# Retention then gated feed-forward: where the third and fourth parts of w_in stand in the hand-written opening

## The chip, the cores and the metric

The kernel runs on one core of one Trainium2 chip. The metric is the device time of one execution in microseconds (us). The kernel before takes 1028.38 us, the median of five runs (1027.11 to 1031.23).

## The reference

```python
# q, k, v: (8 batches, 8 heads, 576 tokens, 64), fp32
scores = q @ k.T / sqrt(64)
ret    = scores * Dmat           # Dmat[i, j] = gamma_h ** (i - j) for i >= j, else 0
x      = ret @ v                 # laid out as (4608 tokens, 512 = heads * 64)
h      = x @ w_in                # w_in: (512, 2048), float64
g      = h * erf(softplus(h))
out    = g @ w_out               # w_out: (2048, 512), float64; out in fp32
```

## The kernel before

**Attention by pieces.** The 4608 tokens are cut into 36 pieces of 128. They are counted from 0 here, as in the code, so "the sixth piece" is piece 5. A piece goes through three stages. `transposes(i)` (L315), here Ti, turns q and then k on TensorE against `ident` (into `pt_q`, `pt_k`, L332), has ScalarE copy both to SBUF (`qT`, `kT`), has GpSimd weigh v (L313), and asks for q of piece i+2. `scores(i)` (L341), here Si, multiplies k by q (L347), and VectorE masks the result into `sT`. `outputs(i)` (L354), here Oi, multiplies `sT` by v (L365), adds what earlier pieces of the batch left (L376), forms the new state (L388), has VectorE scale and sum (`x`, `sums`) and GpSimd scale the state (L427), and asks for k and v of piece i+3. A load of q, k or v of one piece is two DMAs of 128 KB (L147), so a piece is 768 KB.

**Feed-forward by chunks.** Four pieces make a chunk of 512 tokens. The first chunk is multiplied by the first group of w_in columns in the plain way: `plain()` (L539) has 16 steps, four for each quarter of the 512 rows of w_in, and a step is four matmuls (L550, into `p`, `p`, `pe`, `pg`). The steps of a quarter need the part of w_in with these rows, already rounded. Later chunks use a Strassen-like scheme (L496, L604).

**Weights.** w_in and w_out come as float64 words. `load_weights()` (L232) asks for the next part: of w_in, 512 KB in two DMAs of 256 KB on SyncE's queue (L237), into one of four buffers `wraw`. `round_weights(n)` takes n steps of `rounding()` (L240), which turns one part into fp32 in `wa`. The first step is two instructions on ScalarE (L254, L255), the next three are one instruction each on VectorE (L259, L263, L267), and the fifth is three (L272, L274, L275), on VectorE too for the first group of w_in. So "5" rounds one part.

**Queues.** Each engine runs its instructions in the order in which the code issues them, and SyncE issues its DMAs in that order; nothing is rescheduled. Eight completion semaphores go round among the DMAs, so that a DMA's issue also waits for the landing of the one eight before it.

**The opening.** A string of letters drives the first chunk (L727): "a" runs the next attention stage, "w" asks for a part of the weights, a digit takes so many rounding steps, "p" is one step of `plain()`, "k" issues two matmuls that keep TensorE busy, and "l", "c", "s" are a load, the rest of the constants and a store of x. With the stages and parts written out, the kernel before runs:

```
T0 l k S0 k T1 k O0 w1 k S1 k T2 k O1 w2 S2 T3 3 O2 w3 w4 S3 2 T4 O3 S4 5 pp T5 pp O4 w5 w6 pp S5 5 pp
O5 w7 5 T6 pp w8 c pp S6 5 pp T7 O6 S7 pp 5 s
```

"3" and "2" round part 1; the following "5"s round parts 2, 3, 4, 5 and 6 (w5 on belongs to w_out). T3 asks for q of piece 5 and O2 for its k and v.

Of the kernel before, what the change touches and what calls it, by code (L numbers as in the profile page):

```python
# [54 lines left out]
def kernel(  # L55
# [94 lines left out]
    def load(i, names="qkv"):  # L150
        if i < len(pieces):
            t = loaded.setdefault(i, {})
            for name in names:
                src = {"q": q, "k": k, "v": v}[name]
                if name == "q" and i < SQUARES:
                    t["q"] = load_rows(i, "q", q, 2)
                elif name == "q":
                    t["qs"] = load_squares(i, "q", q)
                    if i >= SQUARES_K:
                        t["ks"] = load_squares(i, "k", k)  # L160
                elif name == "v" or i < SQUARES_K or len(pieces[i]) == 1:
                    t[name] = load_rows(i, name, src, 4)
# [69 lines left out]
    def load_weights():  # L232
        part = next(coming, None)
        if part is not None:
            t = wraw.tile([P, 2 * WP], UINT32, tag="wraw", name="wraw")
            for rows, src in part[0]:
                nc.sync.dma_start(out=t[rows].rearrange("p (h f) -> p h f", h=2), in_=src)  # L237
            words.append((t, *part[1:]))
# [49 lines left out]
    def round_weights(n=1):  # L288
        for _ in range(n):
            next(round_step, None)  # L290
# [159 lines left out]
    def attend(upto):  # L450
        while done[0] < min(upto, len(stages)):
            of, i = stages[done[0]]
            of(i)
            done[0] += 1
# [9 lines left out]
    def store_x(c):  # L464
        nc.sync.dma_start(out=xd[c], in_=x[0, c][:, :n_dc])
# [242 lines left out]
    def keep_busy(n):  # L708
        for _ in range(n):
            nc.tensor.matmul(idle[:, :P], lhsT=ones, rhs=ones, start=True, stop=True)  # L710
# [13 lines left out]

    for what in "alkakakawkakakawaa3awwa2aaa5ppappawwppa5ppaw5appwcppa5ppaaapp5s":  # L727
        if what == "a":
            attend(done[0] + 1)
        elif what == "p":  # L730
            next(products)
        elif what == "s":
            store_x(0)
        elif what == "l":
            load(2, "kv")
        elif what == "c":
            nc.sync.dma_start(out=cst[:, CONST_FIRST:], in_=consts[:, CONST_FIRST:])
        elif what == "w":
            load_weights()
        elif what == "k":  # L740
            keep_busy(2)
        else:
            round_weights(int(what))
# [93 lines left out]
```

## Time and profile before

| what | value |
|---|---|
| median of five runs | 1028.38 us |
| the profiled execution's own time | 1027.11 us |
| its span in the profile | 1025.3 us |
| TensorE busy | 1017.5 us, 99% of the span |
| VectorE, ScalarE, GpSimd busy | 65%, 38%, 12% |
| granted TensorE clock | 0.999 |
| DMA | 165.76 MB, mean 162 GB/s |

Times in the views are counted from the start of the span. 1.81 us of the profiled execution's time lie outside its span. "Busy" is the time that an engine spends in instructions; the timeline joins equal instructions into one row with its start, its length and, in brackets, how long the engine sat idle before it and what ended that. A row of TensorE (PE) that is longer than others of its kind hides a wait between its instructions. SPq is the issuing of DMAs by SyncE; a DMA lands some us after its issue.

### The profile page before, as it was taken

How to read it: one execution, taken by the hardware profiler on the slowest of the kernel's cores; microseconds unless marked ns; L12 is line 12 of the kernel's file. 1: busy time of each engine (PE TensorE's matmuls, PEld its weight loads, DVE VectorE, ACT ScalarE, POOL GpSimd, SP SyncE). 2: the span in 40 equal slices, each digit the busy share in tenths (PEclk: the TensorE clock that was granted, in tenths of full speed). 3: DMA queues.
4: the chain of work that ended last, by engine and by line, in shares of the span. 5: the costliest groups of instructions: out<-in, count | busy, mean ns of one | idle time of the engine just before them, and what ended most of it. 6: DMA issues, size and time to landing. Idle time of an engine off the chain costs nothing.

```text
span 1025.3 us, 15950 instructions
## 1 busy us (share of the span) xinstructions
PE 1017.5 (99%) x6348; PEld 876.2 (85%) x6348; DVE 669.6 (65%) x1055; ACT 390.4 (38%) x481; POOL 123.4 (12%) x122
## 2 busy tenths in 40 slices
PE   9999999999999999999999999999999999999998
PEld 8787888888788888888888888888888888888887
DVE  3869777977976656656666666666567655555555
ACT  2354133233234444434343444444433333333332
POOL 2143112122312110010001001000100000000000
PEclk9999999999999999999999999999999999999999
DMA  9997989979984344544444345444433334444433
GB/s 196 205 252 165 232 194 224 250 150 251 245 191 159 111 156 145 167 159 154 166 142 165 123 147 164 162 144 144 144 124 124 125 130 132 125 134 136 124 95 112
DMA packets 146986, 165.76 MB, mean 162 GB/s; under 512 B 97376, under 2 KB 121568, under 8 KB 138848
## 3 DMA queue, kind: packets, MB, share of 16 engines
q1 hardware_dynamic: 144848, 163.70, 57.0%
q10 hardware_dynamic: 2064, 1.05, 0.4%
q8 instruction: 50, 0.82, 0.4%
q14 instruction: 24, 0.20, 0.1%
HBM read 117.52 MB, written 47.19 MB: 161 GB/s over the span
## 4 chain that ended last, share of the span: by engine, by line
PE 83%; DMA 6%; DVE 4%; SPq 4%; issue 1%; ACT 1%; POOL 1%; ACTq 0%; DVEq 0%; POOLq 0%
PE a L604 23%; PE a L496 22%; PE g L604 11%; PE g L496 11%; PE e L604 6%; PE e L496 5%; DMA raw_v<-in_v_dram 2%; PE o L365 2%; PE s L347 2%; SPq L131 2%; SPq L147 1%; DMA wraw<-in_moe_w_in_dram 1%; DMA raw_ks<-in_k_dram 1%; PE o L388 1%; PE o L376 1%
## 5 line engine op out<-in xcount | busy, mean ns | idle before, releaser
L496 PE MATMUL a<-x,wa 128*128 128x256 f32 x1088 | 258.3, 380 | 0.0
L496 PEld LDWEIGHTS a<-x,wa 128*128 128x128 f32 x1088 | 205.8, 190 | 28.5
L604 PE MATMUL a<-wb,s 128*128 128x256 f32 x864 | 205.7, 381 | 0.0
L604 PEld LDWEIGHTS a<-wb,s 128*128 128x128 f32 x864 | 162.9, 190 | 23.5 <-ACT o L618 0.7
L99 DVE TENSOR_TENSOR t<-g,t 128x512 f32<-128x512 f32 x68 | 46.9, 690 | 150.4 <-ACT t L526 112.8
L496 PE MATMUL g<-x,wa 128*128 128x256 f32 x544 | 129.2, 380 | 0.0
L496 PEld LDWEIGHTS g<-x,wa 128*128 128x128 f32 x544 | 102.8, 190 | 14.4
L99 DVE TENSOR_TENSOR o<-a,o 128x512 f32<-128x512 f32 x108 | 74.1, 686 | 49.3 <-PE a L604 49.3
L521 ACT COPY t<-a 128x512 f32<-128x512 f32 x34 | 19.9, 585 | 188.2 <-PE a L496 188.2
L99 DVE TENSOR_TENSOR t<-t,s 128x1024 f32<-128x1024 f32 x72 | 88.9, 1274 | 0.0
L565 ACT ACTIVATE s<-t 128x1024 f32<-128x1024 f32 x72 | 72.1, 1049 | 27.4 <-DVE t L99 27.4
L274 POOL TENSOR_TENSOR wraw<-wraw 128x512 f32<-128x512 f32 x28 | 29.4, 1050 | 440.2 <-DVE wraw L272 178.1
L99 DVE TENSOR_TENSOR x<-x 128x512 f32<-128x512 f32 x115 | 75.8, 692 | 1.2
L532 ACT COPY t<-a 128x512 f32<-128x512 f32 x34 | 19.9, 586 | 144.4 <-PE a L496 144.4
L569 ACT ACTIVATE s<-s 128x1024 f32<-128x1024 f32 x72 | 72.1, 1049 | 0.4
L604 PE MATMUL g<-wb,s 128*128 128x256 f32 x288 | 68.6, 381 | 0.1
L604 PE MATMUL e<-wb,t 128*128 128x256 f32 x288 | 68.5, 381 | 0.0
L604 PE MATMUL a<-wb,t 128*128 128x256 f32 x288 | 68.5, 381 | 0.0
L604 PE MATMUL g<-wb,t 128*128 128x256 f32 x288 | 68.2, 380 | 0.0
L496 PE MATMUL e<-x,wa 128*128 128x256 f32 x272 | 64.8, 381 | 0.0
L99 DVE TENSOR_TENSOR o<-g,o 128x512 f32<-128x512 f32 x72 | 49.2, 683 | 23.6 <-ACT o L618 18.8
L99 DVE TENSOR_TENSOR sT<-s,cst 128x512 f32<-128x512 f32 x72 | 46.1, 681 | 27.9 <-PE s L347 27.9
(76 smaller groups left out, 1227.6 us busy)
## 6 DMA issues: line engine op xcount, KB each, us to landing
od<-o SPq DMA_DIRECT2D x54, 512.0 KB, 3.3
x<-xd SPq DMA_DIRECT2D x27, 1024.0 KB, 4.8
o<-od SPq DMA_DIRECT2D x27, 1024.0 KB, 5.0
raw_qs<-in_q_dram SPq DMA_DIRECT2D x96, 112.0 KB, 4.3
raw_ks<-in_k_dram SPq DMA_DIRECT2D x84, 112.0 KB, 4.2
xd<-x SPq DMA_DIRECT2D x9, 1024.0 KB, 5.4
raw_v<-in_v_dram SPq DMA_DIRECT2D x64, 128.0 KB, 4.5
wraw<-in_moe_w_in_dram SPq DMA_DIRECT2D x32, 256.0 KB, 5.6
```

The source lines that it names most:

```text
L99: nc.vector.tensor_tensor(out=out, in0=in0, in1=in1, op=op)
L131: nc.sync.dma_start(out=t[part * SQ : (part + 1) * SQ, :, at : at + m - SQ], in_=tokens[:, :, d0 : d0 + m - SQ])
L147: queue.dma_start(out=t[r0 : r0 + n, e::2, :], in_=heads.rearrange("h p d -> p h d"))
L274: engine.tensor_tensor(out=r_f, in0=high_f, in1=r_f, op=ALU.mult)
L347: nc.tensor.matmul(ps[e][:, p, :], lhsT=t["kT"][heads[e], p, :], rhs=t["qT"][heads[e], p, :], start=True, stop=True)
L365: nc.tensor.matmul(o[p % 2][heads[(e + p) % 2], p // 2, :], lhsT=t["v"][:, 2 * p + e, :], rhs=t["sT"][:, e, p, :], start=(p < 2), stop=(no ...
L496: nc.tensor.matmul(acc[:, j * TH : (j + 1) * TH], lhsT=weights["wa", self.g][:, a, d, j * P : (j + 1) * P], rhs=x[self.g, self.c][a][:, d, :],
L521: nc.scalar.copy(out=self.t1[:, 1], in_=self.a)
L532: nc.scalar.copy(out=self.t2[:, 0], in_=self.a)
L565: nc.scalar.activation(self.s[:, j], t, AF.Softplus)
L569: nc.scalar.activation(self.s[:, j], self.s[:, j], AF.Erf)
L604: nc.tensor.matmul(acc[:, tp, :], lhsT=left[:, j * TH + tp * P : j * TH + (tp + 1) * P], rhs=weights["wb", self.g][:, b, j, :], start=(sta ...
```

## The change

Only the string changes.

```diff
-    for what in "alkakakawkakakawaa3awwa2aaa5ppappawwppa5ppaw5appwcppa5ppaaapp5s":
+    for what in "alkakakawkakakawwaa3awa2aaa5ppappa5wwppa5ppawappwcppa5ppaaapp5s":
```

Written out, the kernel after runs:

```
T0 l k S0 k T1 k O0 w1 k S1 k T2 k O1 w2 w3 S2 T3 3 O2 w4 S3 2 T4 O3 S4 5 pp T5 pp O4 5 w5 w6 pp S5 5 pp
O5 w7 T6 pp w8 c pp S6 5 pp T7 O6 S7 pp 5 s
```

On SyncE's queue the two DMAs of w3 move ahead of the six of piece 5; w4 stays where it was, behind v of piece 5 and ahead of piece 6. On VectorE the rounding of part 3 moves ahead of the masking of S5, and that of part 4 ahead of the scaling of O5. TensorE, ScalarE and GpSimd run the same instructions in the same order as before.

## The prediction

> **What bounds the kernel now.** I read the page first. Its line on the engines settles that TensorE is the bound: it idles for under 8 of 1025.3 us.
>
> ```profile
> PE 1017.5 (99%) x6348; PEld 876.2 (85%) x6348; DVE 669.6 (65%) x1055; ACT 390.4 (38%) x481; POOL 123.4 (12%) x122
> ```
>
> So this change can only take away a wait of TensorE or add one. Next the table of waits for the first 100 us, in which the change lies: line, what was waited for, us in total, times, longest.
>
> ```profile
> PE p L550 <- DVE wa L275: 1.1, 2, 0.8
> ...
> PE s L347 <- DVE qT L326: 0.4, 1, 0.4
> ```
>
> The matmuls of the first chunk wait twice, 1.1 us together, for a rounded part of w_in. The timeline of TensorE says where.
>
> ```profile
> 29.55 1.99 PE L550 MATMUL p<-x,wa 128*128 128x256 f32 x8
> 31.38 0.60 PE L332 MATMUL pt_q<-ident,raw_q 128*128 128x128 f32 x4
> 31.88 0.63 PE L332 MATMUL pt_k<-ident,raw_k 128*128 128x128 f32 x4
> 32.34 1.03 PE L550 MATMUL pe<-x,wa 128*128 128x256 f32 x4
> ...
> 36.03 1.99 PE L550 MATMUL p<-x,wa 128*128 128x256 f32 x8 [0.30 <-DVE wa L275]
> ...
> 40.97 1.09 PE L365 MATMUL o<-sT,raw_v 128*64 128x128 f32 x16
> ...
> 49.60 1.99 PE L550 MATMUL p<-x,wa 128*128 128x256 f32 x8 [0.75 <-DVE wa L275]
> ```
>
> The wait at 36.03 is for part 2, which the change doesn't touch; the one at 49.60 is for part 4. The rows at 31.38 and 31.88 are T5. Its last input is the second DMA of k of piece 5. The timeline of SyncE's queue gives the issues; under them is, from the answer on this tile for the two DMAs of the second row, the time from issue to landing.
>
> ```profile
> 24.98 1.09 SPq L147 DMA_DIRECT2D raw_q<-in_q_dram  x2
> 26.12 1.05 SPq L147 DMA_DIRECT2D raw_k<-in_k_dram  x2
> ```
>
> ```profile
> DMA to landing us min/median/max: 5.1/5.1/5.1
> ```
>
> The second k DMA is issued at 26.67 and, at 5.1 us, lands at 31.8. T5 uses it at 31.88: no slack, and no wait to be seen either, since the matmuls of 29.55 end just before.
>
> **Part by part: the DMA that moves.** w3 (512 KB) goes ahead of q, k and v of piece 5 (768 KB). In this stretch the queue lands its DMAs in the order of issue, at 166 to 226 GB/s by the table of windows, with five or more on the way, so what w3 takes is added to q and k. How much, the parts show. Behind w2 the landings are: w2's second at 29.8 (issue 23.18, 6.6 us), w3's second at 37.0 (31.45, 5.5), w4's second at 39.7 (32.74, 6.9). Before w2, v of piece 4 landed at 27.6 (22.04, 5.5), and before w3 v of piece 5 at 33.4 (29.25, 4.2). So a part takes 2.2 us (w2), 3.6 (w3, asked for late) or 2.7 (w4, straight behind w3). The moved w3 will stand straight behind w2, as w4 stands behind w3: I take 2.7 and keep 2.2 to 3.6. k of piece 5 lands at 34.5 and T5's transposes of k start at 34.6, not 31.88: **+2.7 us**. TensorE runs in order, and behind T5 stand `pe` and `pg`, O4, and all the rest; no other work fills the hole. Later DMAs keep their places: w4 and piece 6 follow as before, and piece 6 had slack (k landed at 41.8, T6 used it at 43.7).
>
> The Trainium skill, "DMA: Bandwidth & Descriptors", section "Specifications", gives 358 GB/s from HBM per core. By that 512 KB would take 1.5 us and the sum below would be 1.2 us smaller; the windows here stay well below it (166 to 226 GB/s), so the row decides.
>
> **The waits that go.** With TensorE 2.7 us later, part 2 is ready in time: **-0.3**. Part 4's rounding now comes before O5's scaling, and at 49.60 it is over long since: **-0.75**. Nothing is late in its place: S6 stands just ahead on TensorE, and its own inputs (T6) are old.
>
> **VectorE's new order.** Here is what the rounding of part 3 costs, and the masking it now precedes (timeline of VectorE).
>
> ```profile
> 36.56 0.41 DVE L99 TENSOR_TENSOR x<-o,cst 128x256 f32<-128x256 f32 x1
> 39.15 1.29 DVE L99 TENSOR_TENSOR sT<-s,cst 128x512 f32<-128x512 f32 x2 [2.18 <-PE s L347]
> 40.35 0.41 DVE L259 TENSOR_SCALAR wa<-wa 128x512 f32<-128x512 f32 x1
> ...
> 43.25 0.69 DVE L275 TENSOR_TENSOR wa<-wa,wraw 128x512 f32<-128x512 f32 x1
> 43.86 0.42 DVE L99 TENSOR_TENSOR x<-o,cst 128x256 f32<-128x256 f32 x1
> ```
>
> The six instructions take 3.5 us (40.35 to 43.86). In the new order they begin after O4's scaling. O4 ends 2.7 us later than before, at 38.4, its scaling at 39.2 (two instructions of 0.41 after it); ScalarE has done part 3's share by then (behind T5's copies, at 36.9). So the rounding fills 39.2 to 42.7, most of which VectorE idled before (2.18 us), and `sT` of S5 comes at 42.7 to 44.0. O5 (40.97, now +2.4) is due at 43.4 and needs both halves, so its second matmul waits until 44.0: **+0.6**. The nearest rows are O2 and O3, where `sT` came 0.36 and 0.49 us after the start and the 16 matmuls took 1.51 and 1.64 us for 1.09. Bounds: 0 to 1.0. Part 4 then fills 44.0 to 47.5; it delays O5's scaling to 48.4, and behind that waits S6, for its PSUM buffers, at 50.6: cover of 2 us. GpSimd's state and the weighing of v of piece 6 move to 48 to 50; O6 needs them at 54.5. ScalarE's two instructions a part keep their order and are short of nothing. If w3 came later than 39, the rounding would push `sT` further, us for us; at 32.5 it is far from that.
>
> **The sum.** +2.7 - 0.3 + 0.6 - 0.75 = +2.25 us at 50 us. From there to the end TensorE waits only 0.36 us at 80.97 and about 0.5 us inside O rows near 87, both for VectorE work whose start goes back over ScalarE (softplus, from 62) to TensorE's own matmuls, so all of it shifts together and gives nothing back. On the profiled execution this is 1027.11 + 2.25 = 1029.4; the median lies 1.27 us above that execution, so 1028.38 + 2.25 = **1030.6 us**. Bounds of the terms: low 2.2 - 0.3 + 0 - 0.75 = +1.15, high 3.6 - 0.3 + 1.0 - 0.75 = +3.55, that is 1029.5 to 1031.9. What a measurement of this kernel can tell from no change is about 0.2%, 2.06 us, 1030.44; the sum lies just above it.
>
> **The clock.** In 25 to 50 us the granted clock is 1.00, in every window, and TensorE never idles more than 0.75 us there. The changed kernel gives it a hole of up to 2.7 us, for which this trace has no row. The nearest is the start, where TensorE comes out of rest: by the timeline the first 20 `idle` matmuls (L710, 128x128) take 4.64 us, 232 ns each, while the later groups of four take 0.61 us, some 140 ns each with the last one's latency spread over them. So a cold stretch there cost at most 20 x 0.09 = 1.8 us. I take no loss, since the hole is split (q's transposes come about 1 us before k's), and keep 1.8 us as the bound.
>
> By the Trainium skill, "TensorE: Matmul & The Clock Gate", section "Part 1: The HAM clock gate", a whole idle window of about 3.4 us halves the clock, and as long a busy one restores it. It speaks against this change: a hole a little longer than the 2.7 us would by an estimate from that page (half of 3.4 us) add some 1.7 us to the sum; a hole of 2.7 us adds nothing.
>
> **Rivals.**
>
> *The stall holds, about as summed* (0.66). For it: k lands 0.1 us before its use and 512 KB go ahead of it. Its range, +1.15 to +3.55 with the scatter of a median of five, is about two thirds above 2.06 us, since the term for w3 has more room upward (2.7 to 3.6) than downward (2.7 to 2.2): 0.45 slower, 0.21 the same.
>
> *The stall is larger* (0.15): the clock falls, or the small packets of q and k run slower behind two parts in a row (the rate fell to 166 GB/s in 30 to 35 us). 2.25 + 1.8, or 3.55 + 1.8: 1032.4 to 1033.7. For it: the slow row at the start. Against it: the clock of 1.00 in every window.
>
> *Not slower* (0.13): the queue has room, and w3 goes into its gaps. At 31 to 32 us the queue moved only 88 GB/s, so there is some. Place: T5's transposes of k. Price: the gain of 1.05 us (0.30 and 0.75) stays and the delay is small. It decides if k of piece 5 lands before 31.88 + 1.05 = 32.9, that is if w3 costs it at most 1.1 us, half of what the cheapest part cost; time 1027.3 to 1028.4. Nearly all of this is within 0.2%.
>
> *Faster by more* (0.06): besides the 1.05 us, TensorE would have to lose its waits inside O2 and O3 (0.42 + 0.55, before the change's place) or those at 80.97 and 87 (0.36 + 0.5): about 1026.4. I see no path from the change to them.
>
> *The change doesn't do what it says* for part 4: its DMAs don't move, so it can be rounded sooner only since they landed at 39.7, before VectorE's new turn at 44.0. That suffices.
>
> **How the numbers follow.** Predicted 1030.6. Slower: 0.45 + 0.15 = 0.60. Same: 0.21 + 0.11 = 0.32; faster: 0.02 + 0.06 = 0.08. The range leaves out the far end of the larger stall and the faster case: 1028.0 to 1033.2.
>
> **What would show it.** Right: TensorE's timeline has a row `pt_q` or `pt_k` with about 2 us of idle time before it at T5, k of piece 5 landing near 34.5; no brackets at the two `p` rows; an O5 row of 1.5 to 1.8 us; everything from 50 us on later by about 2. Wrong: T5 starts within 1 us of 31.9, or O5 starts no later than 41, or the granted clock is below 1 in 31 to 40 us, or a later wait (80.97) shrinks by what T5 lost.

## The result, and the profile after

The changed kernel takes 1030.51 us (median of 24 runs, 1029.17 to 1032.11), the kernel before 1027.93 us (44 runs taken beside them and earlier). The ratio is 1.0026, 95% interval 1.0020 to 1.0032: slower, by 2.7 us (0.0026 x 1028), between 2.1 and 3.3. The profiled execution took 1031.37 us; its span is 1029.6 us, 4.3 us above the one of before. That is more than the medians differ, because the first trace of before is of a quick execution (1027.11 us) and this one is of a late one; the experiments show what makes the difference. Two single executions among the experiments, of 1766.21 us (clock 0.556 throughout) and 3166.01 us, lie far off all others and are left out of every ratio, average and count of clocks.

The page's line on the engines: TensorE is busy 2.2 us longer, with the same 6348 instructions, so some of them took longer.

```profile
PE 1019.7 (99%) x6348; PEld 877.5 (85%) x6348; DVE 667.0 (65%) x1055; ACT 390.1 (38%) x481; POOL 122.5 (12%) x122
```

The table of waits of TensorE in the first 100 us. The wait of L550 for VectorE (1.1 us) is gone; a wait for a DMA, of which there was none, stands first.

```profile
PE pt_q L332 <- DMA raw_q<-in_q_dram: 2.2, 1, 2.2
```

The timeline of TensorE, the rows that answer to those of before.

```profile
29.62 1.99 PE L550 MATMUL p<-x,wa 128*128 128x256 f32 x8
33.78 1.08 PE L332 MATMUL pt_q<-ident,raw_q 128*128 128x128 f32 x4 [2.17 <-DMA raw_q<-in_q_dram]
34.94 1.09 PE L332 MATMUL pt_k<-ident,raw_k 128*128 128x128 f32 x4
35.82 1.68 PE L550 MATMUL pe<-x,wa 128*128 128x256 f32 x4
37.33 1.03 PE L550 MATMUL pg<-x,wa 128*128 128x256 f32 x4
...
39.78 1.99 PE L550 MATMUL p<-x,wa 128*128 128x256 f32 x8
...
44.87 1.64 PE L365 MATMUL o<-sT,raw_v 128*64 128x128 f32 x16
...
53.22 1.99 PE L550 MATMUL p<-x,wa 128*128 128x256 f32 x8
```

T5 stands for 2.17 us until q has landed. Then `pt_q`, `pt_k` and `pe` take 1.08, 1.09 and 1.68 us, against 0.60, 0.63 and 1.03 before, 1.6 us more together. The two brackets at the `p` rows are gone, and O5 takes 1.64 us for 1.09, a wait hidden in its row. These rows make up nearly all of the 2.2 us. Against the first trace of before TensorE is late by 2.4 us at `pt_q`, 3.1 at `pt_k`, 3.75 at the second quarter (39.78 for 36.03), 4.4 at the end of O5 and 3.6 at the fourth quarter (53.22 for 49.60).

The issues, and from the answer on the tile for the second k DMA (issued at 28.25) its time to landing: k lands at 34.7.

```profile
22.60 3.39 SPq L237 DMA_DIRECT2D wraw<-in_moe_w_in_dram  x4
26.09 1.09 SPq L147 DMA_DIRECT2D raw_q<-in_q_dram  x2
27.54 1.68 SPq L147 DMA_DIRECT2D raw_k<-in_k_dram  x2
```

```profile
DMA to landing us min/median/max: 6.4/6.4/6.4
```

VectorE: part 3 (40.57 to 44.08) now precedes the masking of S5, part 4 (45.28 to 48.79) follows it without a gap.

```profile
40.57 0.42 DVE L259 TENSOR_SCALAR wa<-wa 128x512 f32<-128x512 f32 x1
...
43.47 0.69 DVE L275 TENSOR_TENSOR wa<-wa,wraw 128x512 f32<-128x512 f32 x1
44.08 1.28 DVE L99 TENSOR_TENSOR sT<-s,cst 128x512 f32<-128x512 f32 x2
45.28 0.42 DVE L259 TENSOR_SCALAR wa<-wa 128x512 f32<-128x512 f32 x1
...
48.18 0.69 DVE L275 TENSOR_TENSOR wa<-wa,wraw 128x512 f32<-128x512 f32 x1
```

The table of windows: from, to and length; busy time of the five engines; then PEclk, the granted clock, DMA share and GB/s. The clock, 1.00 in every window of before, falls to a half behind the hole.

```profile
32.00:34.00 2.00, 0.22 (x1) 0.25 (x2) 1.83 (x4) 0.00 (x0) 0.00 (x0) 0.93 0.66 124
34.00:36.00 2.00, 1.93 (x9) 1.56 (x9) 0.92 (x2) 0.58 (x1) 0.00 (x0) 0.50 0.75 166
36.00:38.00 2.00, 2.00 (x9) 1.61 (x7) 0.00 (x0) 1.71 (x3) 1.04 (x1) 0.72 0.83 183
38.00:40.00 2.00, 2.00 (x35) 1.64 (x34) 0.53 (x2) 0.00 (x0) 0.00 (x0) 1.00 1.23 184
```

The clock lost is 2 x (0.07 + 0.50 + 0.28) = 1.7 us, a half-speed stretch of 3.4 us.

### The profile page after: what moved, and what is told of

Its sections match the earlier page's. It is cut to its first block, busy times and chain, and to the rows that moved or that the text cites. A ratio compares the mean times of both kernels' runs of the same rounds, so it can differ in the third digit from the quotient of the medians.

```text
span 1029.6 us, 15948 instructions
## 1 busy us (share of the span) xinstructions
PE 1019.7 (99%) x6348; PEld 877.5 (85%) x6348; DVE 667.0 (65%) x1055; ACT 390.1 (38%) x481; POOL 122.5 (12%) x122
## 4 chain that ended last, share of the span: by engine, by line
PE 88%; DMA 5%; DVE 3%; SPq 2%; issue 1%; POOL 1%; ACTq 0%; DVEq 0%; POOLq 0%
PE a L604 23%; PE a L496 22%; PE g L604 11%; PE g L496 11%; PE e L604 6%; PE e L496 5%; PE o L365 2%; PE s L347 2%; SPq L147 1%; PE o L388 1%; PE o L376 1%; DMA raw_ks<-in_k_dram 1%; DMA raw_qs<-in_q_dram 1%; DMA raw_q<-in_q_dram 1%; DVE sT L99 1%
```

## The experiments

Theory Q: w3 in the queue holds up q and k of piece 5, TensorE stands at T5, and in part of the executions its clock then falls. Theory V: VectorE's new order costs the time. Ratios are against the kernel before, run on the same chip.

**The DMAs alone.** The string of before, with w3 asked for beside w2 and the roundings left where they were.

```diff
-...kakakawaa3awwa2aaa5ppappawwppa5ppaw5appwc...
+...kakakawwaa3awa2aaa5ppappawwppa5ppaw5appwc...
```

> Only the DMAs of part 3 move ahead of piece 5; the rounding stays where it was before the change. Theory Q (the queue: q and k of piece 5 come late, TensorE stands at T5 and in part of the executions its clock then falls): T5 stands about 2.2 us before pt_q as in the changed kernel (k of piece 5 landing near 34.7), O5 is not stretched (1.1 us, not 1.64), the wait for part 4 at the fourth quarter is between 0 and 0.7 us; in all +2.0 to +2.8 us, ratio 1.0020 to 1.0027. Theory V (VectorE: the rounding ahead of S5's masking and O5's scaling is what costs): no loss, ratio 1.000.

Measured: ratio 1.0034 (1.0022 to 1.0046), median 1031.68 us of 5 runs. TensorE's timeline:

```profile
33.64 0.63 PE L332 MATMUL pt_q<-ident,raw_q 128*128 128x128 f32 x4 [1.92 <-DMA raw_q<-in_q_dram]
34.84 0.63 PE L332 MATMUL pt_k<-ident,raw_k 128*128 128x128 f32 x4 [0.57 <-DVE wa L275]
...
43.55 1.09 PE L365 MATMUL o<-sT,raw_v 128*64 128x128 f32 x16
...
52.19 1.99 PE L550 MATMUL p<-x,wa 128*128 128x256 f32 x8 [0.76 <-DVE wa L275]
```

The hole is there and O5 is not stretched, as Q says; V is out as the main cause. (The bracket at `pt_k` names VectorE, which was done at 34.7; k landed at 34.6.) The loss lies above the range I gave. The wait at the fourth quarter stayed whole, since VectorE's chain shifted along with TensorE; and four of the five runs had a mean clock of 0.998 or less. The trace is of the one that had not (1030.09 us); `pt_q` and `pt_k` ran at full speed in it.

**The rounding alone.** The DMAs as before, the two "5"s one stage sooner.

```diff
-...aaa5ppappawwppa5ppaw5appwc...
+...aaa5ppappa5wwppa5ppawappwc...
```

> Only the rounding moves one stage ahead; the DMAs stay as before, so part 3 lands at 37.0. Theory Q: T5 runs at 31.4 without a wait; the rounding of part 3 waits for its landing and ScalarE (38.3), ends at 41.9, S5's masking ends at 43.1, so O5 (due at 40.97) is about 2.1 us late; the wait of 0.75 for part 4 goes: +1.35 us, ratio 1.0013. Theory V: the whole loss is here, ratio 1.0025. If rounding sooner is simply a gain: -0.75 us, ratio 0.9993.

Measured: ratio 1.0023 (1.0013 to 1.0033). The interval just reaches the 1.0013 that I gave for Q and holds V's 1.0025, so the ratio by itself does not decide between the two. In the trace O5 waits and is stretched, and the fourth quarter waits no more.

```profile
42.10 1.64 PE L365 MATMUL o<-sT,raw_v 128*64 128x128 f32 x16 [0.35 <-issue]
...
50.45 1.99 PE L550 MATMUL p<-x,wa 128*128 128x256 f32 x8
```

Against the first trace of before TensorE is late by 0.70 us at the second quarter, 1.68 at the end of O5 and 0.85 at the fourth quarter: +0.98 and -0.83, so the new order by itself costs 0.15 us there. (The 0.70 is older than the change: T4 already starts 0.86 us later in this execution.) 5 of the 12 runs had a mean clock of 0.996 to 0.998; they average 1031.8 us, the other seven 1028.9. The trace is of one of the seven, so where the clock falls in the five is not shown. The seven average 1.0 us above the kernel before (1028.0); the trace does not show where that arises, since its span of 1027.4 us is also that of the third trace of before (below).

**Part 3 behind k.** The changed kernel, with w3 asked for between k and v of piece 5.

```diff
-...kakakawwaa3awa2...
+...kakakawaa3awa2...
-        load(i + 3, "kv")
+        load(i + 3, "k")
+        if i == 2:
+            load_weights()
+        load(i + 3, "v")
```

> The changed kernel with part 3 asked for between k and v of piece 5 instead of ahead of q. Theory Q: T5 runs at 31.9 at full clock, part 3 lands near 35, its rounding fills 36.9 to 40.4, S5's masking ends at 41.6 and O5 loses 0.6 us; the wait of 0.75 for part 4 goes, that of 0.3 for part 2 stays: -0.15 us, ratio 0.9995 to 1.0003. Theory V: the loss stays, ratio 1.002.

Measured: ratio 1.0005 (0.9996 to 1.0013), no run with a mean clock under 0.999. The loss of the change is gone, though the roundings stand where the change puts them. This is the run that decides against V, since it has VectorE's order of the changed kernel.

```profile
31.60 0.63 PE L332 MATMUL pt_q<-ident,raw_q 128*128 128x128 f32 x4 [0.22 <-DMA raw_q<-in_q_dram]
32.94 0.63 PE L332 MATMUL pt_k<-ident,raw_k 128*128 128x128 f32 x4 [0.71 <-DMA raw_k<-in_k_dram]
...
42.65 1.64 PE L365 MATMUL o<-sT,raw_v 128*64 128x128 f32 x16 [0.92 <-issue]
```

O5 lost more than the 0.6 us that I gave: TensorE is 0.69 us behind the first trace of before at the second quarter, 2.23 behind O5 and 1.40 at the fourth quarter, so here VectorE's order costs 1.5 and gives back 0.8. Most of the excess is one instruction of part 3's rounding: L267 took 1.53 us from 38.42 (0.69 in the changed kernel), while GpSimd weighed v of piece 5 (38.36 to 39.40), the load that w3 stands ahead of here. T5 still waits for k, a microsecond later than in the first trace of before, with nothing moved ahead of k. That asked for further traces of before (below).

**Both parts ahead.** The changed kernel, with w4 asked for beside w2 and w3: twice the bytes ahead of q and k.

```diff
-...kakakawwaa3awa2...
+...kakakawwwaa3aa2...
```

> The changed kernel with part 4 too ahead of piece 5: twice the bytes that hold q and k up. Theory Q: q and k of piece 5 come another 2.3 to 2.7 us later (k near 37.2), T5 stands for 4.5 us, the clock falls in nearly all runs (means of 0.997 to 0.998); +5 to +6.5 us, ratio 1.0049 to 1.0063. Theory V (VectorE's order, which is that of the changed kernel): ratio 1.0026.

Measured: ratio 1.0063 (1.0050 to 1.0076), all of the runs compared at a mean clock of 0.996 or 0.997.

```profile
35.84 1.09 PE L332 MATMUL pt_q<-ident,raw_q 128*128 128x128 f32 x4 [3.94 <-DMA raw_q<-in_q_dram]
36.99 1.09 PE L332 MATMUL pt_k<-ident,raw_k 128*128 128x128 f32 x4
```

k landed at 36.9, 2.2 us after the changed kernel's 34.7: the second part costs what the first did. The loss grows with the bytes, as Q says; V, with the changed kernel's order, gave 1.0026.

**The hole filled.** The changed kernel with matmuls that nothing reads just ahead of T5, 14 in the first run and 8 in the two others, to hold the clock while q and k are awaited.

```diff
+        elif what == "b":
+            for _ in range(14):
+                nc.tensor.matmul(firsts[0].acc[3][:, :P], lhsT=ones, rhs=ones, start=True, stop=True)
-...aaa5ppappa5ww...
+...aaa5ppbappa5ww...
```

> The changed kernel with 14 matmuls of 128x128 on ones (into the bank of pg, before its first use) put just ahead of T5, to fill the 2.2 us in which TensorE stands. If the fall of the clock behind the hole is a part of the loss: the granted clock stays at 1.00 in 32 to 38 us, the pt_q, pt_k and pe rows go back to about 0.6, 0.6 and 1.0 us, runs above 1031 us vanish, ratio 1.0016 to 1.0019 (the hole itself stays). If the clock plays no part: ratio 1.0026 as in the changed kernel; more if the added matmuls delay T5.

> The changed kernel with 8 instead of 14 matmuls in the hole ahead of T5, since 14 took 3.1 us and held T5 up past the landing of q. The clock stays at 1.00 (no run with a mean under 0.999), T5 starts at 33.8, when q lands: ratio 1.0015 to 1.0020. If the clock plays no part: 1.0026.

> The changed kernel with 8 matmuls in the hole once more, for a trace at full clock and a narrower ratio. If the clock is about half of the loss: pt_q, pt_k and pe rows of 0.6, 0.6 and 1.0 us, no mean clock under 0.999, ratio 1.0010 to 1.0020. If not: 1.0026.

Measured: 1.0025 (1.0016 to 1.0034) with 14; 1.0013 (1.0002 to 1.0024) and 1.0013 (1.0004 to 1.0022) with 8. In all 31 runs compared no mean clock is under 0.999. From the trace of the third (T4 was late by 1 us there, so the hole is shorter):

```profile
34.15 0.60 PE L332 MATMUL pt_q<-ident,raw_q 128*128 128x128 f32 x4
35.33 0.63 PE L332 MATMUL pt_k<-ident,raw_k 128*128 128x128 f32 x4 [0.58 <-DVE wraw L274]
```

```profile
34.00:36.00 2.00, 1.42 (x12) 1.20 (x12) 1.81 (x3) 0.58 (x1) 0.00 (x0) 1.00 0.76 162
36.00:38.00 2.00, 2.00 (x15) 1.52 (x14) 0.00 (x0) 1.72 (x3) 1.04 (x1) 1.00 0.85 178
```

Filled, the hole leaves the clock at 1.00, and k's lateness stays (it landed at 34.9 and 35.1 in the two traces). The averages are 1030.4, 1029.7 and 1029.7 us; the changed kernel's own 13 runs at 0.999 or more average 1029.9, its 12 at 0.998 or less 1031.4. So where the clock falls it costs 1.4 us, and it falls in about half of the executions. With 14 matmuls T5 starts only at 34.6, 0.8 us after q has landed, so little could be gained. The two ratios with 8 are lower than the changed kernel's 1.0026, but their intervals overlap its 1.0020 to 1.0032; that filling gives time back is likely, not shown. That it keeps the clock up is plain in all three.

**Second and third traces of before, second of after.** The same kernels once more.

> The kernel before once more, for a second trace of it: 1027 to 1029 us. It tells which differences between traces come from one execution to the next: the start of T4 (24.4 or 25.2) and the wait of S for kT near 271 (0.41 in the first trace, 0.9 in all five later ones). If these change here too, they are no part of the change; if kT's wait is 0.4 again, the shift of TensorE makes it longer, and 0.5 us of the loss arise there.

> The kernel before for a third trace. If the first trace was a lucky one at T5 (k of piece 5 landed at 31.75 there, at 32.96 in the second): k lands at 32.5 to 33.1 and T5 waits for it by about 1 us. If the second was the unlucky one: 31.8 again.

> The changed kernel for a second trace: k of piece 5 lands at 34.5 to 34.9 in any case; the clock either falls behind T5 (rows of 1.1 and 1.7 us, about 1031.4 us) or stays (0.6 and 1.0 us, about 1029.8 us).

The kernel before took 1028.92 and 1029.15 us. The second trace, one row; then the third:

```profile
33.09 0.63 PE L332 MATMUL pt_k<-ident,raw_k 128*128 128x128 f32 x4 [0.42 <-DMA raw_k<-in_k_dram]
```

```profile
31.73 0.63 PE L332 MATMUL pt_q<-ident,raw_q 128*128 128x128 f32 x4 [0.29 <-DMA raw_q<-in_q_dram]
32.80 0.63 PE L332 MATMUL pt_k<-ident,raw_k 128*128 128x128 f32 x4 [0.45 <-DMA raw_k<-in_k_dram]
...
50.15 1.99 PE L550 MATMUL p<-x,wa 128*128 128x256 f32 x8 [0.76 <-DVE wa L275]
```

k of piece 5 landed at 32.96 and 32.66, not at 31.75, and T5 waited. So it did in both traces of the split rounding (below), whose DMAs are those of before: 0.44 and 0.43 us at `pt_k`. The trace that the prediction read was a lucky one: in these four T5 costs 0.6 to 1.0 us more than there, and the wait of 0.30 at the second quarter is absent. The wait of S for kT near 271 was 0.4 and 0.9 in these two traces, so it varies by execution and is no part of the change. The changed kernel's second trace (1032.38 us) has k landing at 34.6 and the clock falling again:

```profile
33.68 0.63 PE L332 MATMUL pt_q<-ident,raw_q 128*128 128x128 f32 x4 [2.19 <-DMA raw_q<-in_q_dram]
34.84 1.09 PE L332 MATMUL pt_k<-ident,raw_k 128*128 128x128 f32 x4 [0.53 <-DVE wa L275]
```

**The rounding split.** The DMAs as before; VectorE's idle time before S5's masking takes two instructions of part 3 instead of six, and three of part 4 stay behind O5's scaling. This is what the traces point to: the gain at the fourth quarter without O5's stretch or T5's hole.

```diff
-...aaa5ppappawwppa5ppaw5appwc...
+...aaa5ppappa3wwppa6ppa1wappwc...
```

> The DMAs stay as before the change; the rounding is split: two VectorE instructions of part 3 ahead of S5's masking, the rest of part 3 and three instructions of part 4 behind it, the last three of part 4 behind O5's scaling. By theory Q with the terms of the sum: S5's masking at 39.3 (not delayed), O5 not stretched, part 4 ready at 47.4, so the wait of 0.75 at the fourth quarter goes and nothing takes its place: -0.75 us, ratio 0.9993 (0.9987 to 0.9999). If any rounding ahead of the masking costs as much as in the run with the rounding alone: ratio 1.001 to 1.002.

> The split rounding once more, since its interval (0.9993 to 1.0016) leaves open whether it gains the 0.75 us and how often its clock falls. By the terms of the sum: ratio 0.9993 to 0.9999, and no more runs with a mean clock under 0.999 than the kernel before has (1 in 20). If the low clocks of the first set (3 of 12) belong to it: again about a quarter of the runs, and no gain in the mean.

Measured: 1.0005 (0.9993 to 1.0016) and, again, 0.9994 (0.9984 to 1.0004). The trace of the second:

```profile
41.27 1.09 PE L365 MATMUL o<-sT,raw_v 128*64 128x128 f32 x16
...
49.08 1.99 PE L550 MATMUL p<-x,wa 128*128 128x256 f32 x8
```

O5 is not stretched and the fourth quarter does not wait; from the second to the fourth quarter TensorE gains 0.82 us on the trace of before, in both traces. It beats the changed kernel. That it beats the kernel before is not shown: both intervals hold 1. Low clocks (0.997 and 0.998) came in 3 of the first 12 runs and in none of the next 11; I don't know their cause.

## Why the prediction was right

The time fell where it was said to (1030.5 for 1030.6, inside 1028.0 to 1033.2), and slower was the likeliest case. That the medians meet within 0.1 us is partly luck. The change cost 2.6 us by the medians (2.7 by the ratio) where the sum had 2.25, and the kernel before came out at 1027.93 us, 0.45 below the five-run median from which the prediction counted; the two nearly cancel. Inside the sum, T5 was put about 0.3 us too high and the clock 0.7 too low.

**T5: right in kind, over-sized.** The mechanism is shown from four sides: the DMAs alone bring the hole, w3 behind k takes the loss away, a second part doubles k's delay, and the rounding alone has no hole. w3 took 2.2 us by k's landing (34.65, the mean of the changed kernel's two traces, less 32.46, the mean of before's three), not 2.7 (238 GB/s: nearer to the row that was taken than to the 1.5 us estimated from the 358 GB/s of the Trainium skill, "DMA: Bandwidth & Descriptors", "Specifications"). A fault as large lay in the starting point: "no slack, and no wait" was read from one execution, in which k landed 1.2 and 0.9 us sooner than in the other two.

**The waits that go: half right.** The 0.75 at the fourth quarter was there in all three traces of before and went (0.82 in the trace). The 0.30 at the second quarter was there to be gained in the first of the three traces only.

**O5: right.** +0.6 was said; it lost 0.69 us (3.75 to 4.44 behind before). With the 0.82, VectorE's new order nets -0.13 us at the fourth quarter; in the run with the DMAs alone the 0.76 stayed. With w3 behind k the same order cost 0.7 us net, since that one rounding instruction took 0.84 us longer there. The cover for S6 (2 us) held: it started at 52.13, O5's scaling having ended at 49.9.

**The clock: wrong, and it was named.** The step that failed is "I take no loss, since the hole is split", and one of the signs of being wrong that the prediction gave came: a granted clock below 1 in 31 to 40 us. The clock fell in both traces of the changed kernel and, by the mean clocks, in 12 of 25 runs; with the hole filled, or w3 behind k, in none of 42. Its price of 1.4 us is within the bound of 1.8 that was kept as a rival; as a mean over the runs it is 0.7 us. That the bound fits is luck in part: it came from slow matmuls at the start, where the profile gives a granted clock of 1.00 (0 to 5 us), so nothing here shows that the clock made them slow. The Trainium skill's rule ("TensorE: Matmul & The Clock Gate", "Part 1: The HAM clock gate") set the limit at an idle window of about 3.4 us; here 2.17 us of idle time was enough in one trace and 2.19 followed by 0.53 in the other, and with 3.94 us of it the clock fell in every run compared. The measurement decides. The other half of the rule holds: the half-speed stretch lasted 3.4 us in each of the three traces that show one.

**The sum as it stands now.** From the run with the DMAs alone at full clock, TensorE is 2.58 us late at the second quarter; before's three traces are at 0, 0.84 and 0.54, 0.46 in the mean: +2.1. VectorE's order -0.1, the clock +0.7: +2.7 us, against 2.7 measured. The first two terms rest on one trace each; the runs bear them out, since the changed kernel's 13 at full clock average 2.0 us above the kernel before (1029.9 for 1028.0).

That nothing is given back after 50 us held as far as these traces tell: later differences of 0.3 to 1 us (near 250 and 271) came and went between executions of the kernel before alone.

## What to carry to other kernels

Before a load is moved ahead on a queue, look up the landing and the first use of each load that it passes; a load that lands just when it is used has no cover, and here 512 KB in front of it came back as some 2 us of waiting on the engine that runs in order. A single trace can hide such a wait: a landing 0.1 us before its use in one execution was 0.4 us of waiting in the next, so read a tight spot in two or three traces before its price is worked out. The hole of about 2 us in TensorE's work cost another 1.4 us in about half of the executions, in the clock behind it; 8 or 14 matmuls that nothing reads, put into it, kept the clock up in all 31 runs here.

## What was not expected of the hardware

The clock's fall after so short a hole (2.17 us idle, and 2.19 and 0.53, in the two traces where it fell; 1.92 and 0.57 us in the one of the DMAs alone where it did not) was the surprise. What sets whether it falls is not settled: the two kinds of execution differ by a few tenths of a microsecond of idle time, and where the clock fell in the runs with only the rounding moved (5 of 12) and in the first with the rounding split (3 of 12), which have no such hole in their traces, no trace shows.
